# Four of thirty-two weight pieces converted in slots 21 and 22 of a fused attention and MLP kernel

## The chip, the cores and the metric

The kernel runs on one core of one Trainium2 chip. The metric is the device time of one execution in microseconds (us), as the median of several runs; lower is better. Beside it stands one profiled execution, recorded instruction by instruction.

## The reference, cut to what matters

```python
# q, k, v: (8, 8, 576, 64) float32; tau = 0.02
scores = (1 / sqrt(64)) * q @ k.transpose(0, 1, 3, 2)
thresh = max(scores, -1) - tau
scores = where(scores >= thresh, scores, -1e9)
attn = exp(scores - max(scores, -1))
attn = attn / (sum(attn, -1) + 1e-9)
x = (attn @ v) -> rows (b, s), columns (h, d): (4608, 512)
h = x @ w_in                 # (512, 2048), float64 as handed over
g = 0.5 * h * (1 + erf(h / sqrt(2)))
out = g @ w_out              # (2048, 512), float64 as handed over
```

The two weight matrices reach the kernel as 64-bit floats. [...] every weight element is turned from 64 to 32 bits on the chip, once, by integer operations on the two 32-bit halves of each number.

## The kernel before, in words

**Slots.** The attention is cut into pairs of heads: p = 0 to 31, four pairs to a batch. A pair has five score chunks, i = 0 to 4: four of 128 query rows for each of the two heads, and a last one (i = 4, `NC`) with the 64 rows left over from both. One chunk of one pair is a slot, n. Slots 0 to 7 hold chunks 0 and 1 of pairs 0 to 3, slots 8 to 19 their chunks 2 to 4, and from slot 20 (`BATCH`) on each pair has five slots in a row. The main loop (L1137 to L1257) goes through the slots and issues the instructions of each in an order written out by hand; nothing is reordered later, each engine works its own list from front to back.

**A slot.** `scores` (L391) puts four matmuls into two PSUM tiles `sc` (one tile when i = 4); there are two such tiles in all, so the scores of slot n+1 need the tiles of slot n to have been read. `softmax_head` (L403) has, for each of the two heads e, VectorE's row maximum `nmx` (L412), GpSimd's threshold `thr` (L415) and ScalarE's exponential `p` (L417). `softmax_tail` (L420) multiplies by the mask on VectorE (L433), which is also the last reader of `sc`. The probabilities are then turned. For the first four pairs TensorE does it (L347, copied out by ScalarE at L354 and L362); from slot 20 on VectorE does (L532 or L530), followed by DMAs that regroup (L550, L554). `turn_qk` (L372; L382, L383, L388 on VectorE), issued at i = 2, turns q and k of the next pair, after ScalarE scaled q (L370, at i = 1). `weigh_v` (L571) multiplies with v into `xT`; ScalarE copies it to a block of x (L589).

**The MLP between.** 256 rows of x make a block. `fill` (L695) puts matmuls of the MLP of blocks 0 to 7 into the slots as soon as there is credit for them: layer 1 (L671, `hT` from w_in), GELU on ScalarE, then layer 2 (L686, `o_ps` from `g` and w_out, j = 0 to 15 in turn, twice for the two halves of a block). A matmul is only issued when the weight pieces it needs have been converted in the program's order (`converted`, L707). Until slot 20 ScalarE only copies layer 1's results out (L638); the GELU of these, held back, runs in slot 20 (`gelus_held`, L648), and the first `o_ps` matmuls stand in slots 21, 22 and 23. The last ten blocks are done after the attention, with fewer multiplications (L859).

**Weight pieces.** There are 32 pieces of 128 x 512 elements (512 KB each, raw): 16 of w_in, then 16 of w_out, so that piece 16 + j is row block j of w_out. One conversion step of a piece is:

- an SP DMA that loads the raw piece (`load_piece`, L161), every second one into one of the seven x slots of `xall`, the others into `turned_p`, about eight pieces ahead;
- two ScalarE activations (`convert_first`, L196: `power` at L199 and the part in the weight at L200), done one piece ahead of the rest;
- two VectorE operations (`convert_second`, L203: L207 and L208), after which the next raw piece is loaded;
- one GpSimd addition (`add_low_bits`, L215, L219), which makes the weight ready. In the next slot it is issued for the newest piece between the first head's `nmx` and the first `thr` (L414), and for older pieces after the slot's head (L1144).

`STEPS` (L1129) says how many steps stand at the end of each slot (L1231); it adds up to 32 by slot 18. The tiles `power` come from the pool `gp` with ten buffers, which also holds `g`, the outputs of layer 1. Before the last slots of the first batch `convert_ahead` (L1173) issues ScalarE's part early. `LATER` is the number of last pieces that always go to x slots, because `turned_p` is needed for its own purpose from slot 20. `keep_busy` (L1239) adds a few idle matmuls in slots 1, 6 and 8.

## Time and profile before

| | |
|---|---|
| median of 3 runs | 1331.73 us (1331.51 to 1331.79) |
| the profiled execution's own time | 1331.37 us |
| its span | 1329.2 us |
| TensorE busy | 1315.9 us, 99% |
| VectorE busy | 1040.7 us, 78% |
| ScalarE busy | 604.3 us, 45% |
| GpSimd busy | 635.2 us, 48% |
| VectorE L207, one piece | median 423 ns, least 416, most 962 |
| VectorE L208, one piece | median 693 ns, most 1646 |
| ScalarE L199, one piece | about 705 ns |
| GpSimd L219, one piece | about 1272 ns |

The 2.2 us between the profiled execution's span and its own time lie outside the span. Busy times are sums over the whole span; the engines depend on each other, so the stretch that the change touches, from slot 2 (18.65 us after the start) to slot 24 (147 us), has to be looked at by itself. In the records two instructions that follow each other overlap a little: L207 and L208 take 0.42 and 0.69 us each, and two steps together 2.13 us. A 32-bit matmul shows as two records.

### The profile page before, as it was taken

The page shows a single profiled execution, that of the slowest core. Times are in us where ns is not written, and L with a number is a line of the kernel's source. Part 1 is how long each engine was busy: PE and PEld are TensorE (multiplying, and loading weights), DVE is VectorE, ACT ScalarE, POOL GpSimd, SP SyncE. Part 2 cuts the span into 40 slices and gives each one's busy share as a digit, 9 for nine tenths or more (in the row PEclk, how much of TensorE's full clock was granted, in tenths as well). Part 3 has the DMA queues.
Part 4 walks back from the last instruction along what each step waited for, and adds up shares of the span by engine and source line. Part 5 has one row for each costly group of instructions (what it writes and reads, how often), then busy time and mean ns, then how long its engine had stood idle before and what let it go on. Part 6 is the DMA issues. An engine that isn't in the chain of part 4 may idle for free.

```text
span 1329.2 us, 19865 instructions
## 1 busy us (share of the span) xinstructions
PE 1315.9 (99%) x6306; PEld 891.0 (67%) x6306; DVE 1040.7 (78%) x2001; ACT 604.3 (45%) x1027; POOL 635.2 (48%) x1058
## 2 busy tenths in 40 slices
PE   9999999999999999999999999999999999999998
PEld 6766466476476466466466466468778787877877
DVE  6887787788888888888888888883857698386674
ACT  7987356367367358358458338232111203211120
POOL 3555445555655655655655641236264403645430
PEclk9999999999999999999999999999999999999999
DMA  8553666777877887787787775500000140000003
GB/s 260 166 179 88 141 150 160 169 162 159 191 170 156 192 186 157 193 198 162 184 207 159 176 174 108 106 9 0 1 0 1 40 105 15 0 1 0 1 0 79
DMA packets 213687, 153.14 MB, mean 115 GB/s; under 512 B 117264, under 2 KB 196992, under 8 KB 213584
## 3 DMA queue, kind: packets, MB, share of 16 engines
q1 hardware_dynamic: 195440, 125.31, 40.7%
q0 software_dynamic: 17712, 26.26, 7.6%
q8 instruction: 52, 0.85, 0.3%
q14 instruction: 51, 0.42, 0.1%
q10 hardware_dynamic: 432, 0.30, 0.1%
HBM read 56.62 MB, written 12.58 MB: 52 GB/s over the span
## 4 chain that ended last, share of the span: by engine, by line
PE 93%; DVE 3%; ACT 2%; issue 1%; DMA 0%; POOL 0%; DVEq 0%; ACTq 0%; POOLq 0%
PE bank L859 34%; PE o_ps L686 17%; PE hT L671 16%; PE sc L400 13%; PE xT L571 11%; DVE nmx L412 1%; ACT p L417 1%; DVE power L208 1%; DVE p L433 1%; DVE power L207 1%; PE tr L347 1%; DMA q<-in_q_dram 0%; ACT pT L354 0%; PE tr L317 0%; PE idle L147 0%
## 5 line engine op out<-in xcount | busy, mean ns | idle before, releaser
L417 ACT ACTIVATE p<-sc,nmx 128x576 f32<-128x576 f32 x288 | 201.9, 737 | 280.9 <-DVE nmx L412 280.7
L433 DVE SCALAR_TENSOR_TENSOR p<-sc,thr,p 128x576 f32<-128x576 f32 x288 | 225.3, 816 | 72.6 <-ACT p L417 66.1
L415 POOL TENSOR_SCALAR thr<-nmx,tau_eff 128x1 f32<-128x1 f32 x288 | 83.9, 293 | 340.2 <-DVE nmx L412 338.1
L671 PE MATMUL hT<-xall,w_in 128*128 128x256 f32 x1024 | 241.9, 386 | 0.0
L412 DVE TENSOR_REDUCE nmx<-sc 128x1 f32<-128x576 f32 x288 | 205.4, 750 | 44.9 <-PE sc L400 43.7
L686 PE MATMUL o_ps<-w_out,g 128*128 128x512 f32 x512 | 236.8, 603 | 0.2 <-ACT g L644 0.2
L671 PEld LDWEIGHTS hT<-xall,w_in 128*128 128x128 f32 x1024 | 189.7, 190 | 51.1 <-issue 24.5
L741 DVE TENSOR_TENSOR o<-o,bank 128x256 f32<-128x256 f32 (+1 forms) x242 | 100.2, 418 | 94.3 <-PE bank L859 89.3
L741 DVE TENSOR_TENSOR c<-c,bank 128x320 f32<-128x320 f32 x304 | 147.1, 488 | 34.2 <-PE bank L859 21.0
L686 PEld LDWEIGHTS o_ps<-w_out,g 128*128 128x128 f32 x512 | 93.2, 190 | 109.5 <-issue 106.7
L400 PE MATMUL sc<-kT,qT 64*128 64x288 f32 x960 | 160.5, 429 | 1.9 <-DVE p L433 1.2
L571 PE MATMUL xT<-pT,v 128*64 128x320 f32 (+1 forms) x1240 | 159.4, 410 | 0.2
L532 DVE STREAM_TRANSPOSE turned_p<-p 128x1152 f32<-128x1152 f32 x112 | 154.4, 1378 | 3.9
L400 PEld LDWEIGHTS sc<-kT,qT 64*128 64x128 f32 x960 | 91.9, 186 | 75.8 <-issue 60.8
L571 PEld LDWEIGHTS xT<-pT,v 128*64 128x64 f32 x1240 | 86.4, 137 | 70.8 <-issue 11.1
L859 PE MATMUL bank<-w_out,c 128*128 128x256 f32 (+1 forms) x484 | 120.5, 380 | 0.8 <-DVE o L741 0.8
L260 POOL DMA_DIRECT2D v<-in_v_dram x208 | 110.8, 536 | 3.7 <-issue 1.6
L859 PEld LDWEIGHTS bank<-w_out,c 128*128 128x128 f32 x484 | 90.4, 190 | 18.8 <-DVE o L741 3.2
L926 ACT ACTIVATE c<-c 128x320 f32<-128x320 f32 (+1 forms) x80 | 46.9, 624 | 115.0 <-DVE c L741 114.9
L859 PE MATMUL bank<-t_out,g 128*128 128x256 f32 (+1 forms) x324 | 82.5, 377 | 0.4 <-DVE o L741 0.4
L859 PE MATMUL bank<-t_out,c 128*128 128x256 f32 x320 | 82.8, 381 | 0.0
L741 POOL TENSOR_TENSOR c<-c,g 128x320 f32<-128x320 f32 (+1 forms) x40 | 50.5, 1271 | 67.5 <-DVE c L741 67.5
(185 smaller groups left out, 1751.2 us busy)
## 6 DMA issues: line engine op xcount, KB each, us to landing
pT<-turned_p SPq DMA_DIRECT2D x448, 160.0 KB, 3.6
pT<-pd_tail SPq DMA_DIRECT2D x112, 80.0 KB, 3.0
q<-in_q_dram POOLq DMA_DIRECT2D x104, 72.0 KB, 3.6
k<-in_k_dram POOLq DMA_DIRECT2D x104, 72.0 KB, 3.3
inv<-turned SPq DMA_DIRECT2D x54, 128.0 KB, 4.1
v<-in_v_dram POOLq DMA_DIRECT2D x156, 40.0 KB, 3.1
out_dram<-o SPq DMA_DIRECT2D x40, 128.0 KB, 2.4
xall<-in_moe_w_out_dram SPq DMA_DIRECT2D x9, 512.0 KB, 4.7
```

The lines of the kernel that those rows point to most:

```text
L260: eng.dma_start(t[r:P:4, e, 0:n, :], rows[:, r * KR:r * KR + n, :])
L400: nc.tensor.matmul(sc[e][:, h, 0:HALF], lhsT=lhsT, rhs=s["kT"][rows, at:at + HALF], start=True, stop=True)
L412: nc.vector.tensor_reduce(nmx[:, e:e + 1], sc, axis=AXIS.XY, op=ALU.max, negate=True)
L415: nc.gpsimd.tensor_scalar(thr[:, e:e + 1], nmx[:, e:e + 1], -1.0, tau_eff, op0=ALU.mult, op1=ALU.subtract)
L417: nc.scalar.activation(w[:, e * S:(e + 1) * S].rearrange("p (h s) -> p h s", h=2), sc, AF.Exp, bias=nmx[:, e:e + 1], scale=1.0)
L433: nc.vector.scalar_tensor_tensor(row, sc[e][:, :, 0:HALF], thr[:, e:e + 1], row, op0=ALU.is_ge, op1=ALU.mult, accum_out=den[e])
L532: nc.vector.transpose(turned_p[:, :, i // 2, 0:NB, i % 2 * Q:(i % 2 + 1) * Q], w.rearrange("p (e b i) -> p e b i", e=2, i=Q))
L571: nc.tensor.matmul(to, lhsT=s["v"][:, e, c, :], rhs=rhs, start=(c == 0), stop=(c == KR - 1))
L671: nc.tensor.matmul(hT[:, j % 2, :], lhsT=w_in_sb[c][:, j * P:(j + 1) * P], rhs=x_blk[n][:, c, :], start=(c == 0), stop=(c == N_DM - 1))
L686: nc.tensor.matmul(o[:, 0:d_model], lhsT=g[j][:, m * P:(m + 1) * P], rhs=w_out_sb[j], start=(j == 0), stop=(j == N_DF - 1))
L741: eng.tensor_tensor(out, a, b, op=ALU.add)
L859: nc.tensor.matmul(to, lhsT=l, rhs=r, start=start and k == 0, stop=k == len(pairs) - 1, skip_group_check=not start)
```

## The change

It does four things. `STEPS` loses the step of slot 2 and that of slot 4, and one of the two steps in slot 6 and in slot 18; the other slots up to 18 keep their number. The four steps are put at the end of slots 21 and 22, two each; in these ScalarE's part is no longer done ahead (`ahead_of` = 0), so that each piece goes through its ScalarE and VectorE operations before the next one begins. `LATER` becomes 4: pieces 28 to 31 are loaded into x slots and stay raw there. `load_piece` remembers loads that found no free x slot and makes up for them later. In the program as built TensorE's list of instructions is the same before and after; the lists of the other engines differ in the places of the conversion steps and of their loads.

```diff
-    LATER = 2
+    LATER = 4
...
+    wanted = [0]
...
     def load_piece(eng=nc.sync):
-        k = loaded[0]
-        if k == len(pieces):
-            return
-        staged = k % 2 and k < len(pieces) - LATER
-        if wide and not staged and not x_free:
-            return
...
+        wanted[0] += 1
+        while wanted[0] > 0 and loaded[0] < len(pieces):
+            k = loaded[0]
+            staged = k % 2 and k < len(pieces) - LATER
+            if wide and not staged and not x_free:
+                return
...
+            wanted[0] -= 1
...
-    def convert(steps):
+    def convert(steps, ahead_of=1):
 
         while steps > 0 and (ahead or raws):
-            convert_ahead(1)
+            convert_ahead(ahead_of)
             convert_second()
             steps -= 1
...
-    STEPS = [0, 1, 1, 1, 1, 1, 2, 1, 2, 2, 2, 2, 3, 2, 2, 3, 2, 2, 2]
+    STEPS = [0, 1, 0, 1, 0, 1, 1, 1, 2, 2, 2, 2, 3, 2, 2, 3, 2, 2, 1, 0, 0, 2, 2]
...
-            convert_ahead(STEPS[n] if n < BATCH - 1 else LATER)
+            convert_ahead(STEPS[n])
...
-        convert(STEPS[n] if n < BATCH - 1 else len(pieces))
+        convert(STEPS[n] if n < len(STEPS) else 0, 1 if n < BATCH else 0)
```

More of the change, by code (lines that the diff above doesn't have):

```diff
@@ L155 @@
     wide = moe_w_in.dtype != FP32
-    LATER = 2
+    LATER = 4
     raws = []
     loaded = [0]
+    wanted = [0]
     converted = [0]
     def load_piece(eng=nc.sync):
-        k = loaded[0]
-        if k == len(pieces):
-            return
-        staged = k % 2 and k < len(pieces) - LATER
-        if wide and not staged and not x_free:
-            return
-        dst, src = pieces[k]
-        loaded[0] += 1
-        if not wide:
-            nc.sync.dma_start(dst, src)
-            converted[0] += 1
-            load_piece()
-            return
-        slot = []
-        if staged:
-            half, at = divmod(k // 2 % 4, 2)
-            raw = pd[half].bitcast(U32)[:, at * 2 * PIECE:(at + 1) * 2 * PIECE]
-        else:
-            slot = [x_slot()]
-            raw = x_rows(slot[0]).bitcast(U32)
-        eng.dma_start(raw, src.bitcast(U32))
-        raws.append((dst, raw, slot))
+        wanted[0] += 1
[4 more added lines that the diff above has]
+                return
+            dst, src = pieces[k]
+            loaded[0] += 1
+            if not wide:
+                nc.sync.dma_start(dst, src)
+                converted[0] += 1
+                continue
+            wanted[0] -= 1
+            slot = []
+            if staged:
+                half, at = divmod(k // 2 % 4, 2)
+                raw = pd[half].bitcast(U32)[:, at * 2 * PIECE:(at + 1) * 2 * PIECE]
+            else:
+                slot = [x_slot()]
+                raw = x_rows(slot[0]).bitcast(U32)
+            eng.dma_start(raw, src.bitcast(U32))
+            raws.append((dst, raw, slot))
     ahead = []
```

## The prediction

> **What bounds the kernel now.** I read the page first, then TensorE's busy time by stretch, then the timeline of the slots that the change touches. The page has TensorE at 99% over the span:

> ```profile
> PE 1315.9 (99%) x6306; PEld 891.0 (67%) x6306; DVE 1040.7 (78%) x2001; ACT 604.3 (45%) x1027; POOL 635.2 (48%) x1058
> ```

> So only time in which TensorE stands still can be won, and any new standstill is lost for good, because its list runs in a fixed order. Where it stands still is in the table of stretches (start and end in us, then busy time of TensorE, of its weight loads, VectorE, ScalarE, GpSimd):

> ```profile
> 42.00:60.00 18.00, 17.12 (x153) 13.12 (x153) 16.79 (x36) 16.60 (x37) 9.91 (x15) 1.00 0.49 159
> 60.00:80.00 20.00, 18.62 (x102) 13.45 (x101) 16.42 (x35) 17.18 (x35) 10.45 (x13) 1.00 0.52 138
> 100.00:118.00 18.00, 16.53 (x93) 11.64 (x92) 15.81 (x32) 14.20 (x30) 11.30 (x15) 1.00 0.52 136
> ...
> 130.00:141.00 11.00, 11.00 (x31) 4.89 (x30) 6.67 (x12) 7.67 (x13) 5.10 (x11) 1.00 0.28 61
> 141.00:147.00 6.00, 6.00 (x19) 2.73 (x19) 5.71 (x12) 1.41 (x2) 3.64 (x8) 1.00 0.99 191
> ```

> From 42 to 118 us (slots 7 to 18) VectorE and ScalarE are nearly as full as TensorE and TensorE has gaps. From 130 us on (slots 21 to 24) TensorE has none, and in the last row VectorE is busy 5.71 of 6 us: slots 22 and 23 have no room on VectorE. Slots 2 to 6 are another case. In TensorE's own table it works 16.91 of 17 us there:

> ```profile
> 25.00:42.00 17.00, 16.91 (x168) 1.00 0.76 268
> ```

> The timeline shows slot 6 passing into slot 7 on VectorE (start, length):

> ```profile
> 42.81 0.42 DVE L207 TENSOR_SCALAR power<-power 128x512 uint32<-128x512 uint32 x1
> 43.27 0.69 DVE L208 SCALAR_TENSOR_TENSOR power<-turned_p,power 128x512 uint32<-128x512 uint32 x1
> 43.88 0.42 DVE L207 TENSOR_SCALAR power<-power 128x512 uint32<-128x512 uint32 x1
> 44.33 0.69 DVE L208 SCALAR_TENSOR_TENSOR power<-xall,power 128x512 uint32<-128x512 uint32 x1
> 44.94 1.42 DVE L412 TENSOR_REDUCE nmx<-sc 128x1 f32<-128x576 f32 x2
> ```

> Two steps cost 44.94 - 42.81 = 2.13 us, 1.06 each, and the maximum follows without a gap: here VectorE sets the pace. And slots 21 to 24:

> ```profile
> 135.11 0.82 DVE L433 SCALAR_TENSOR_TENSOR p<-sc,thr,p 128x576 f32<-128x576 f32 x1 [4.08 <-ACT p L417]
> 136.71 1.38 DVE L532 STREAM_TRANSPOSE turned_p<-p 128x1152 f32<-128x1152 f32 x1
> 137.95 2.84 PE L686 MATMUL o_ps<-w_out,g 128*128 128x512 f32 x6
> 138.01 1.39 DVE L412 TENSOR_REDUCE nmx<-sc 128x1 f32<-128x576 f32 x2
> 140.72 1.79 PE L400 MATMUL sc<-kT,qT 64*128 64x288 f32 x8
> 141.20 1.38 DVE L532 STREAM_TRANSPOSE turned_p<-p 128x1152 f32<-128x1152 f32 x1
> 142.45 4.56 PE L686 MATMUL o_ps<-w_out,g 128*128 128x512 f32 x10
> 144.24 1.42 DVE L412 TENSOR_REDUCE nmx<-sc 128x1 f32<-128x576 f32 x2
> 146.84 1.21 PE L400 MATMUL sc<-kT,q_tail 128*128 128x288 f32 x4
> ```

> VectorE idled 4.08 us (a wait for ScalarE, which runs the held-back GELUs) and then has no gap up to 145.6. Slot 23's scores take 1.79 us where eight such records take 1.24 elsewhere: they wait on VectorE's mask already.

> [...] nothing fills VectorE's 4.08 us from behind the waiting mask. [...] L207 has a median of 423 ns and took 962 at 48.24 us, beside a GpSimd multiplication. [...] the largest gap of TensorE between 42 and 160 us is 0.9 us, at clock 1.00.

> **The change part by part.**

> *Slots 2 and 4, one step less each.* VectorE's two operations (21.96 to 23.03 in slot 2) lie in front of a maximum that starts at 23.48 and waits for TensorE's scores (22.20 to 23.44). ScalarE's part (24.16 to 25.31) holds slot 3's exponential back by about 1.0 us, but what that releases, slot 4's scores, stands behind `xT`, `tr` and transposes that keep TensorE busy from 23.53 to 29.1. Slot 4 repeats it (`xT` at 34.05, scores at 38.42). Value: 0. Bounds: 0 to 0.4 us, the small gaps in the records from 21 to 42 us; it cannot be a loss, since work only leaves.

> *Slot 6, two steps to one.* The maximum of slot 7 could start at 43.88, but its scores (43.19, behind the idle matmuls) allow it 1.27 us after their start, as in slots 3 and 5 (22.20 to 23.48, 32.73 to 34.00): 44.46, won 0.48. Then GpSimd: in slot 7 it has one addition instead of two (1.27 us). The first, at 45.17, held the threshold until 46.42 and the mask until 46.76, 1.82 after the maximum; an undelayed mask comes 1.64 after it (39.69 to 41.33). The addition now ends at 45.4: mask at 46.10, won 0.66. The second held the multiplication L498 until 48.18, and this L207 for 0.96 us instead of 0.42. Now L498 can end near 47.7, L207 and L208 at 48.7, and slot 8's maximum starts at 48.75 instead of 49.84. The scores permit it: they wait for the mask too. Won by slot 8: 1.1 us. From there to slot 17 every slot keeps its number of steps, and the gaps above are waits on VectorE, ScalarE and GpSimd, so all move forward together: 1.1 us. Bounds: 0.4 (only the first part) to 1.8 (about one more such collision in ten slots).

> *Slot 18, two steps to one.* VectorE's part (117.21 to 118.28) ended 0.57 us before the next maximum, which waited on TensorE's scores. ScalarE still converts one piece there ahead of the copies (115.79, piece 28 instead of 31), so TensorE's 0.91 us wait for `pT` stays. Value 0, bounds 0 to 0.3.

> *Loads and raw pieces.* Their SP loads keep their sequence and their distance to use. The last is issued behind the q, k and v loads of pair 5, which SP issues from 110.7 to 120.8; such a load lands in about 4.7 us and is used near 143. The four x slots held are seven less the three blocks of batch 0; the next block needs one in slot 27, at 164. Cost 0.

> *Slot 21, two steps added.* After the transpose of 136.71, at 138.01, come 2.13 us of steps (ScalarE's part for the second, 1.15 us, runs from 136.3 on an engine idle until 138.76). The maximum of slot 22 moves from 138.01 to 140.14. The addition for the newest piece, 1.27 us, starts with it, so the mask follows after 1.75 instead of 1.6: 141.9 to 143.4. Slot 23's scores need it and end at 144.7 instead of 142.45: TensorE has six records (2.84 us) in slot 22 and stands still for 2.3 us.

> *Slot 22, two steps added.* From the transpose at 143.5 on, the 3.04 us that lie between 141.20 and 144.24 (L532 and q and k of the next pair) and then 2.13 of steps: maximum of slot 23 at 148.7. ScalarE's parts, waiting for additions until about 143.5, take 2 x 1.15 and end at 145.8, before VectorE reaches them at 146.5. On GpSimd the addition for piece 31 takes 148.9 to 150.1, two thresholds 0.5, and only then comes the one for piece 30: 150.6 to 151.9. TensorE's ten records in slot 23 are j = 11 to 15, two each at 0.43; after j = 13 (147.3) it waits for piece 30 (j = 14) until 152.0. Behind it in TensorE's list are j = 15 and slot 24's scores: these start at 152.0 + 4 x 0.43 = 153.7 instead of 146.84. Delay 6.9 us. VectorE then is on time, so the 0.7 us that slot 25's scores (150.56) lose to a mask falls away: 6.2. GpSimd's k, q and v loads for pair 6 move back some 4 to 5 us; they are used five slots later: 0.

> Bounds of the loss: 4 (additions beside other work, half the last wait) to 7.5 (a VectorE and GpSimd collision in each slot). Apart from that, TensorE stands still for 4.7 us in one piece. [...] I take 0 and keep up to 3 for the range.

> *Sum:* 6.2 - 1.1 = 5.1 us. Against the profiled execution: 1329.2 + 5.1 + 2.2 outside the span = 1336.5. Its 1331.37 lies 0.36 under the median of 1331.73, so in medians 1336.8.

> **The rivals.**

> *The clock falls* in the 4.7 us gap: the same, and about 2.7 more, 1339.5. [...]

> *The last addition isn't what TensorE waits for.* Then slot 24's scores wait for the mask of slot 23 alone, near 151.3: 4.5 - 0.7 - 1.1 = 2.7, 1334.4, on the border to no change. For: one order on GpSimd decides. Against: thresholds stand before that addition in its list.

> *The steps are hidden (faster).* VectorE idles 4.08 us before 135.11. If the 2 x 2.13 us of steps fell into that, or TensorE had work queued beyond the next scores, nothing would be lost and 1.1 to 2 us won: 1330.2. The place is slot 22: it decides if TensorE's work there (2.84 us) is longer than VectorE's way from one scores to the next. It is not: 138.01 to 141.09 was already 3.1 us. Against it also the fixed order: the steps stand behind the mask that waits.

> *The change moves less than it says.* If TensorE's list had been rearranged around the late pieces, layer 2 would simply come later. The built program's list is unchanged, so the waits are real: 1331.7 otherwise.

> **How the numbers follow.** About 0.2% (2.7 us) is what a measurement of this kernel can tell from no change. Forecast 0.60; clock falls 0.18; border case 0.12, half of it slower; hidden 0.05; no effect 0.05. Slower: 0.60 + 0.18 + 0.06 = 0.84; same: 0.06 + 0.05 = 0.11; faster 0.05. The range runs from 1333.8 (loss of 4, gain of 1.8) to 1340.0 (loss of 6.2 to 7.5 with a fallen clock); the two left-out cases, and the ends of the others, are under 2 in 10.

> **What would show it.** The maximum of slot 8 near 48.75; slot 20 earlier by about 1.1. In slots 21 to 24, moved forward by that: TensorE idle about 2 us before slot 23's scores (released by VectorE L433) and 4 to 5 us in slot 23's `o_ps` (released by GpSimd's addition), the rest of the kernel unchanged but later by 5. I am wrong if that second wait is under 2 us, if slot 8 has not moved, or if the early slots 2 to 6 move by over half a microsecond.

## The result, and the profile after

Times are medians of the runs of one chip; the kernel before was run beside the other each time.

| | before | after |
|---|---|---|
| median, us (lowest to highest, runs) | 1331.64 (1330.61 to 1331.79, 6) | 1337.89 (1336.92 to 1339.11, 6) |
| ratio to before, 95% interval | 1 | 1.0049 [1.0036, 1.0062] |
| profiled execution, us | 1331.37 | 1337.85 |
| span, us | 1329.2 | 1335.9 |
| mean granted TensorE clock | 0.999 | 0.997 |

The change costs 6.25 us; the forecast was 5.1 us (1336.8), the range 1333.8 to 1340.0. All line numbers of the kernel after are one higher than before (L412 is L413).

The page's line of busy times says almost nothing: TensorE is at 99% in both, and its sum has risen by 3.1 us. The fall of the clock shown further down is of that size: about 3.2 us.

```profile
PE 1319.0 (99%) x6306; PEld 890.5 (67%) x6306; DVE 1039.1 (78%) x2001; ACT 604.8 (45%) x1027; POOL 635.7 (48%) x1058
```

**The early part.** TensorE by stretch, kernel after (start and end, then busy time of TensorE, weight loads, VectorE, ScalarE, GpSimd; near the end the clock):

```profile
25.00:42.00 17.00, 16.92 (x168) 12.41 (x164) 11.89 (x26) 14.53 (x33) 7.29 (x14) 1.00 0.60 220
42.00:60.00 18.00, 17.60 (x158) 13.99 (x158) 16.49 (x36) 16.46 (x36) 8.76 (x14) 1.00 0.37 117
60.00:80.00 20.00, 18.23 (x100) 13.09 (x99) 16.07 (x33) 16.22 (x33) 10.46 (x13) 1.00 0.54 144
```

Slots 3 to 6 are where they were (16.92 of 17 us against 16.91). From 42 to 60 us TensorE has 0.48 us less of gaps, and from 60 to 80 us it has 0.39 us more again. VectorE's timeline shows the gain arise. Before:

```profile
46.76 0.82 DVE L433 SCALAR_TENSOR_TENSOR p<-sc,thr,p 128x576 f32<-128x576 f32 x1 [0.33 <-POOL thr L415]
...
48.24 0.96 DVE L207 TENSOR_SCALAR power<-power 128x512 uint32<-128x512 uint32 x1
49.23 0.69 DVE L208 SCALAR_TENSOR_TENSOR power<-turned_p,power 128x512 uint32<-128x512 uint32 x1
49.84 1.41 DVE L412 TENSOR_REDUCE nmx<-sc 128x1 f32<-128x576 f32 x2
```

After:

```profile
44.47 1.42 DVE L413 TENSOR_REDUCE nmx<-sc 128x1 f32<-128x576 f32 x2 [0.51 <-PE sc L401]
...
46.10 0.82 DVE L434 SCALAR_TENSOR_TENSOR p<-sc,thr,p 128x576 f32<-128x576 f32 x1
...
47.59 0.62 DVE L208 TENSOR_SCALAR power<-power 128x512 uint32<-128x512 uint32 x1
48.24 0.69 DVE L209 SCALAR_TENSOR_TENSOR power<-xall,power 128x512 uint32<-128x512 uint32 x1
48.84 1.41 DVE L413 TENSOR_REDUCE nmx<-sc 128x1 f32<-128x576 f32 x2
```

The maximum of slot 7 now waits for the scores (44.47; forecast 44.46), the mask is at 46.10 (as forecast), L208 (L207 before) takes 0.62 us, with a GpSimd multiplication (L499) beside it up to 47.92, instead of 0.96 with the same one (L498 before) beside it up to 48.92, and slot 8's maximum is at 48.84 instead of 49.84.

**Slots 21 to 24.** TensorE's timeline (start, length, and in brackets the idle time before the group and what ended it):

```profile
137.32 2.84 PE L687 MATMUL o_ps<-w_out,g 128*128 128x512 f32 x6
142.26 3.00 PE L401 MATMUL sc<-kT,qT 64*128 64x288 f32 x8 [2.10 <-DVE p L434]
145.18 5.00 PE L687 MATMUL o_ps<-w_out,g 128*128 128x512 f32 x6
151.38 1.98 PE L687 MATMUL o_ps<-w_out,g 128*128 128x512 f32 x4 [1.20 <-POOL w_out L220]
153.20 1.13 PE L401 MATMUL sc<-kT,q_tail 128*128 128x288 f32 x4
```

Two standstills that the kernel before did not have: 2.10 us for VectorE's mask, 1.20 us for the addition on GpSimd. Slot 24's scores stand at 153.20 instead of 146.84. GpSimd's own list shows the order that makes the second one: the addition for piece 31, two thresholds, and only then the one for piece 30.

```profile
148.28 1.26 POOL L220 TENSOR_TENSOR w_out<-power,w_out 128x512 uint32<-128x512 uint32 x1 [1.66 <-DVE power L209]
149.53 0.57 POOL L416 TENSOR_SCALAR thr<-nmx,tau_eff 128x1 f32<-128x1 f32 x2
150.07 1.25 POOL L220 TENSOR_TENSOR w_out<-power,w_out 128x512 uint32<-128x512 uint32 x1
```

And the stretches show something that the profile before has nowhere between its first and its last microseconds: the granted clock (third number from the end) falls.

```profile
140.00:142.00 2.00, 0.16 (x1) 0.00 (x0) 1.59 (x3) 1.75 (x3) 2.00 (x4) 1.00 0.94 174
142.00:143.00 1.00, 0.74 (x3) 0.33 (x3) 0.97 (x5) 0.98 (x3) 1.00 (x2) 0.87 0.91 236
143.00:149.00 6.00, 6.00 (x12) 2.92 (x12) 5.89 (x11) 1.20 (x3) 4.34 (x7) 0.50 0.60 140
149.00:150.00 1.00, 1.00 (x2) 0.10 (x1) 0.59 (x2) 1.00 (x2) 1.00 (x3) 0.72 0.00 0
```

Half clock from 142.73, just after the first standstill, for 6.83 us. That is why six `o_ps` records took 5.00 us instead of 2.84 and slot 23's scores 3.00 us: TensorE looks busy from 143 to 149 (6.00 of 6 us), but at a granted clock of 0.50.

**Where the time is.** Start of a slot's scores on TensorE, after minus before:

| slot | 0 | 8 | 9 | 12 to 22 | 23 | 24 | 26 | 81 | 111 | 131 |
|---|---|---|---|---|---|---|---|---|---|---|
| us | +0.04 | -0.46 | -1.00 | -0.63 | +1.53 | +6.36 | +5.64 | +5.94 | +6.10 | +6.77 |

So 1.0 us is won by slot 9, 0.63 of it kept; 6.99 us is lost from slot 22 to slot 24, 0.72 comes back by slot 26; and 1.1 us more slips in later, in slots whose instructions the change does not touch.

### The profile page after: what moved, and what is told of

Read it like the earlier page. It is cut to its first block, busy times and chain, and to the rows that moved or that the text cites. A ratio compares the mean times of both kernels' runs of the same rounds, so it can differ in the third digit from the quotient of the medians.

```text
span 1335.9 us, 19863 instructions
## 1 busy us (share of the span) xinstructions
PE 1319.0 (99%) x6306; PEld 890.5 (67%) x6306; DVE 1039.1 (78%) x2001; ACT 604.8 (45%) x1027; POOL 635.7 (48%) x1058
## 4 chain that ended last, share of the span: by engine, by line
PE 89%; DVE 3%; ACT 3%; DMA 2%; issue 1%; SPq 1%; POOL 1%; DVEq 0%; POOLq 0%; ACTq 0%
PE bank L860 34%; PE hT L672 16%; PE o_ps L687 15%; PE sc L401 12%; PE xT L572 10%; ACT p L418 1%; DVE nmx L413 1%; DMA inv<-turned 1%; PE tr L348 1%; DVE p L434 1%; DMA turned<-turned 1%; ACT pT L355 0%; DVE power L209 0%; DVE power L208 0%; DVE turned_p L533 0%
## 5 line engine op out<-in xcount | busy, mean ns | idle before, releaser
L413 DVE TENSOR_REDUCE nmx<-sc 128x1 f32<-128x576 f32 x288 | 205.3, 749 | 53.0 <-PE sc L401 51.8
```

The source lines that it names most:

```text
L413: nc.vector.tensor_reduce(nmx[:, e:e + 1], sc, axis=AXIS.XY, op=ALU.max, negate=True)
```

## The experiments

Three theories are tested. *The wait (A):* the steps at the end of slots 21 and 22 fill VectorE and GpSimd, TensorE waits for the mask and for the last addition, and the half clock lies under that wait and costs nothing. *The clock (B):* the fall of the clock is part of the cost. *The x slots (C):* four raw pieces kept in x slots press on what comes later. Unless said otherwise an edit is made to the kernel after. Profiles do not all start alike (slot 0 lies up to 0.7 us earlier or later); where it matters the offset is taken off, and said.

**e1: the first standstill filled.** Twelve records of idle matmuls at the end of slot 22.

```diff
-    BUSY = {1: 2, 6: 2, 8: 2}
+    BUSY = {1: 2, 6: 2, 8: 2, 22: 3}
```

> The changed kernel with twelve records of idle matmuls (1.7 us) at the end of slot 22, where TensorE waits 2.1 us for the mask. They should hold the clock at 1.00 there. Theory A (TensorE's start of slot 24 is set by VectorE's steps and then by the last GpSimd addition, and the half clock is hidden under that wait): o_ps of slot 23 takes 2.6 to 2.9 us for its first six records instead of 5.0, the wait for the addition grows from 1.2 to about 4 us, slot 24's scores start within 0.4 us of 153.2, and the total stays within 0.1% of the changed kernel's 1337.9, or up to 2 us above it if the longer wait brings the clock down later. Theory B (the half clock is what costs beyond the mask): slot 24 starts 2 us earlier or more, total 1336 or less.

Measured: 1339.97 us (1338.66 to 1341.31), ratio 1.0059 [1.0044, 1.0074]. TensorE's timeline:

```profile
140.41 1.50 PE L298 MATMUL idle<-ident 128*128 128x128 f32 x12
142.68 1.95 PE L401 MATMUL sc<-kT,qT 64*128 64x288 f32 x8 [0.77 <-DVE p L434]
144.55 2.84 PE L687 MATMUL o_ps<-w_out,g 128*128 128x512 f32 x6
151.80 3.78 PE L687 MATMUL o_ps<-w_out,g 128*128 128x512 f32 x4 [4.41 <-POOL w_out L220]
155.38 2.13 PE L401 MATMUL sc<-kT,q_tail 128*128 128x288 f32 x4
```

At full clock the six `o_ps` records take 2.84 us, and the wait for the addition is 4.41 us, not 1.20. So the second wait was there in the kernel after, too: the half clock had stretched the matmuls in front of it into it. The sum agrees: (3.00 - 1.95) + (5.00 - 2.84) = 3.21 us, and 4.41 - 1.20 = 3.21 us. But here the clock fell in the second standstill (147.39 to 151.80; half clock from 150.63, for 6.83 us), and nothing covers what comes behind it: four records take 3.78 us instead of 1.98, and slot 24 stands 1.8 us later than in the kernel after (8.53 less 0.43 of offset, against 6.32).

**e2: both standstills filled.** As e1, and 20 records of idle matmuls before j = 14 of slot 23.

```diff
+    if n == 0 and m == 0 and j == 14:
+        keep_busy(5)
...
-    BUSY = {1: 2, 6: 2, 8: 2}
+    BUSY = {1: 2, 6: 2, 8: 2, 22: 3}
```

> The changed kernel with twelve records of idle matmuls at the end of slot 22 and twenty (2.9 us) ahead of j = 14 in slot 23, so that both waits of TensorE are filled and the clock should stay at 1.00 throughout. Theory A (the delay is VectorE's and GpSimd's; the clock adds to it only where it falls in the open): slot 24's scores start as late as in the changed kernel, within 0.4 us of 153.2, and the total is 1337 to 1338; less spread between runs than in the kernel with the first filling alone, and about 2 us faster than it. Theory B (the clock costs the time): 1335 or less.

Measured: 1338.41 us (1337.4 to 1339.3), ratio 1.0049 [1.0035, 1.0063]; in the profile the clock stays at 1.00 from 6.96 us until 1.7 us before the end.

```profile
144.46 2.84 PE L689 MATMUL o_ps<-w_out,g 128*128 128x512 f32 x6
147.14 2.39 PE L298 MATMUL idle<-ident 128*128 128x128 f32 x20
151.72 1.98 PE L689 MATMUL o_ps<-w_out,g 128*128 128x512 f32 x4 [2.18 <-POOL w_out L220]
153.54 1.13 PE L401 MATMUL sc<-kT,q_tail 128*128 128x288 f32 x4
```

Slot 24 is 6.69 us late, less 0.27 of offset 6.42: the same as in the kernel after (6.32), without any fall. The loss is made by VectorE and GpSimd alone, as A has it, and where the fall lies under the wait it costs nothing. Slot 24 starts 1.7 us sooner than in e1, where the fall lay in the open; the medians point the same way (6.7 us over the kernel before, against 7.9 in e1), with overlapping intervals.

**e3: both additions ahead of the thresholds in slot 23.**

```diff
+                if (p, i) == (HP, 3):
+                    add_low_bits(True)
```

> The changed kernel with both GpSimd additions of slot 23 ahead of the first threshold. Theory A: piece 30 is ready near 150.8 minus 0.5, so before TensorE has come to it (150.2 at the half clock) or just about; the wait of 1.2 us falls to under 0.3, but the mask comes 1.2 us later (151.1 to 152.6); slot 24's scores start near 152.2 instead of 153.2, total about 1 us less than the changed kernel, 1336.9. Theory B (the clock sets the time): no change in the start of slot 24 beyond 0.2 us. A third view, that the mask and not the addition is last: slot 24 starts later by about 1 us.

Measured: 1337.23 us (1336.23 to 1339.54), ratio 1.0036 [1.0024, 1.0049]. The wait for the addition is 3.85 us where it is 4.4 with full clock otherwise; it ends 0.6 us sooner (150.30 plus 0.46 of offset, against 151.38). The expected wait of under 0.3 us took over the half clock of the profile after; in this run the clock held through the first standstill. The medians lie 0.7 us under the kernel after, with overlapping intervals; in the profile the order of the two additions is worth about what the two thresholds take (0.57 us). The clock fell here, too, from 151.62 for 3.41 us.

**e4: nothing in slot 22.** Pieces 28 and 29 before the mask of slot 21 (VectorE's 4.08 us of idle time in the kernel before), 30 and 31 at the end of slot 21.

```diff
-    STEPS = [..., 3, 2, 2, 3, 2, 2, 1, 0, 0, 2, 2]
+    STEPS = [..., 3, 2, 2, 3, 2, 2, 1, 0, 0, 2, 0]
+    MID = {21: 2}
+    AHEAD = {19: 1}
...
-        if long:
-            convert_ahead(STEPS[n])
+        if long or n in AHEAD:
+            convert_ahead(AHEAD.get(n, STEPS[n]))
...
+        for _ in range(MID.get(n, 0)):
+            convert_second()
+        if n in MID:
+            add_low_bits()
```

> The changed kernel, with pieces 28 and 29 converted in the middle of slot 21, ahead of its mask, where VectorE idles 4.1 us, and pieces 30 and 31 at the end of slot 21; nothing in slot 22. Theory A: slot 23's scores are late by 2.1 to 2.3 us as in the changed kernel, slot 24 by about 2.3 less the early gain, and of that 0.7 comes back at slot 25; total against the kernel before +1.0 us, 1332.6 (range 1331.8 to 1334, the top if the clock falls for 6.8 us as it did after the same gap of 2.1 us: half of six records and more is then lost in the open). Theory B (clock): the top of that range or above, since nothing hides the half clock here: 1335.

Measured: 1336.15 us (1332.6 to 1338.29, 11 runs), ratio 1.003 [1.0021, 1.0039]: above the range that A was given. The profile is of a run that took 1333.57 us:

```profile
141.78 1.94 PE L401 MATMUL sc<-kT,qT 64*128 64x288 f32 x8 [2.17 <-DVE p L434]
143.65 4.56 PE L687 MATMUL o_ps<-w_out,g 128*128 128x512 f32 x10
148.04 1.21 PE L401 MATMUL sc<-kT,q_tail 128*128 128x288 f32 x4
```

The first standstill is the same 2.2 us, the second is gone, the clock did not fall, and slot 24 is 1.20 us late (1.7 with the offset). The eleven times lie in two groups: 1332.6 and 1333.57, with a mean granted clock of 0.999, and nine from 1335.37 to 1338.29, with 0.996 or 0.997. Half clock for 6.83 us lowers the mean of such a run by 0.0026, so the clock fell in the nine. With no second wait to hide it the fall costs about 3 us (the nine have a median of 1336.23, the two a mean of 1333.1): here B has its part. That it fell after this standstill fits, but is not seen, since only one run has a profile.

**e5: nothing at the end of slot 21, two steps in slot 22.** The rest as in e4.

```diff
-    STEPS = [..., 3, 2, 2, 3, 2, 2, 1, 0, 0, 2, 2]
+    STEPS = [..., 3, 2, 2, 3, 2, 2, 1, 0, 0, 0, 2]
+    MID = {21: 2}
+    AHEAD = {19: 1}
```

> The changed kernel, with pieces 28 and 29 converted in the middle of slot 21 and pieces 30 and 31 at the end of slot 22; nothing at the end of slot 21. Theory A: no wait before slot 23's scores (under 0.3 us), then one long wait of 4 to 5 us for the addition for piece 30 in slot 23 at clock 1.00; slot 24 late by 4.6 less the early gain of 0.6, 0.7 back at slot 25: total against the kernel before +3.3 us, 1334.9 (up to 1338 if the clock falls after that gap, since it is nowhere hidden). Theory B: no long wait.

Measured: 1336.36 us (1335.57 to 1337.76), ratio 1.0033 [1.0021, 1.0045].

```profile
140.44 1.80 PE L401 MATMUL sc<-kT,qT 64*128 64x288 f32 x8
142.17 2.84 PE L687 MATMUL o_ps<-w_out,g 128*128 128x512 f32 x6
149.41 2.88 PE L687 MATMUL o_ps<-w_out,g 128*128 128x512 f32 x4 [4.40 <-POOL w_out L220]
```

Here the first standstill is gone and the second is whole; slot 24 is 5.23 us late (4.8 with the offset), 0.9 of it because the clock fell from 150.36 for 3.41 us (2.88 us for 1.98). So in the profiles slot 22's pair of late steps is the dearer, 3.9 us without the fall against 1.7 in e4. In the medians the two come out alike, because most runs of e4 have a fall in the open.

**e6: slots 2 and 4 alone.** Steps as before except none in slots 2 and 4; the two last pieces go before the mask of slot 21, by the lines of e4 (so in e7 to e12 as well).

```diff
-    LATER = 4
+    LATER = 2
...
-    STEPS = [0, 1, 0, 1, 0, 1, 1, 1, 2, 2, ..., 2, 2, 1, 0, 0, 2, 2]
+    STEPS = [0, 1, 0, 1, 0, 1, 2, 1, 2, 2, ..., 2, 2, 2, 0, 0, 0, 0]
+    MID = {21: 2}
+    AHEAD = {18: 1, 19: 1}
```

> The kernel before with the steps of slots 2 and 4 taken out, and the two last pieces converted in the middle of slot 21, in VectorE's 4.1 us of idling. Theory A (slots 2 to 6 are bound by TensorE): slot 7 and slot 8 start within 0.2 us of before, the total is within 0.4 us of before. Rival (each step taken out of an early slot wins its 1.06 us of VectorE): 2.1 us faster. Also: the kernels built from the changed one lose about 1.1 us between slots 80 and 131; if that comes with the four x slots kept raw, it is not seen here.

Measured: 1331.91 us (1330.54 to 1332.89, 13 runs), ratio 1.0000 [0.9992, 1.0008]; the slots' starts are within 0.2 us of those before. The steps of slots 2 and 4 are worth nothing, and two pieces before slot 21's mask cost nothing that shows.

**e7: slot 6 alone.** One step less in slot 6, the last piece before the mask of slot 21.

```diff
-    LATER = 4
+    LATER = 2
...
-    STEPS = [0, 1, 0, 1, 0, 1, 1, 1, 2, ..., 2, 2, 1, 0, 0, 2, 2]
+    STEPS = [0, 1, 1, 1, 1, 1, 1, 1, 2, ..., 2, 2, 2, 0, 0, 0, 0]
+    MID = {21: 1}
+    AHEAD = {}
```

> The kernel before with one of the two steps of slot 6 taken out, and the last piece converted in the middle of slot 21. Theory A: slot 7 starts 0.5 us earlier, slot 8 1.0 us earlier; of this 0.6 to 1.0 is kept to slot 24 and to the end, total 0.6 to 1.0 us faster (ratio 0.9993 to 0.9995). Rival (the step in slot 6 is hidden as those in 2 and 4): no change.

Measured: 1333.11 us (1332.07 to 1334.22, 13 runs), ratio 1.0010 [1.0002, 1.0019]: slower, a miss. The edit had a flaw: in slot 18 it put two pieces through ScalarE ahead of the copies of `pT`, not one, and TensorE waited for these:

```profile
117.32 0.33 PE L348 MATMUL tr<-ident,p 128*128 128x128 f32 x1 [2.05 <-ACT pT L355]
```

That is 2.05 us instead of 0.91, and the clock fell to half at 118.29 for 3.41 us. A fault of the experiment, but a second place where the fall came after a standstill of 2 us.

**e10: slot 6 again, mended.** All else as e7.

```diff
-    AHEAD = {}
+    AHEAD = {18: 1}
```

> The experiment with slot 6 alone, mended: in slot 18 only one piece goes through ScalarE ahead of the copies of pT, as in the kernel before; the last piece follows at the end of that slot, where ScalarE idles 1.5 us. Theory A: TensorE's wait for pT in slot 18 is 0.9 us again instead of 2.1, the clock doesn't fall there, slot 8 starts 1.0 us earlier and the total is 0.6 to 1.0 us under the kernel before. If the total stays above before, the gain of slot 6 is lost elsewhere.

Measured: 1330.78 us (1329.85 to 1331.82, 21 runs), ratio 0.9989 [0.9983, 0.9996], 1.6 us faster by medians, more than the 0.6 to 1.0 expected. The wait for `pT` is back at 0.9 us, the clock stays; in the profile slot 9 is 1.0 us earlier (0.39, and 0.6 of offset), kept to the end. The gain of slot 6 is real, and in the profile close to the 1.1 us of the forecast.

**e8: slots 6 and 8, one step less each.** Two pieces before the mask of slot 21.

```diff
-    LATER = 4
+    LATER = 2
...
-    STEPS = [0, 1, 0, 1, 0, 1, 1, 1, 2, 2, ..., 2, 2, 1, 0, 0, 2, 2]
+    STEPS = [0, 1, 1, 1, 1, 1, 1, 1, 1, 2, ..., 2, 2, 2, 0, 0, 0, 0]
+    MID = {21: 2}
+    AHEAD = {18: 1, 19: 1}
```

> The kernel before with one of the two steps taken out of each of slots 6 and 8, and the two last pieces converted in the middle of slot 21. Theory A: VectorE sets the pace in slot 8 as well, so a second 1.06 us comes on top: slot 9 about 2 us earlier, total 1.6 to 2.1 us faster than before. Rival (the second step runs into TensorE's or ScalarE's bound): as with slot 6 alone, 0.6 to 1.0.

Measured: **1329.46 us** (1329.11 to 1330.38, 17 runs), ratio 0.9984 [0.9976, 0.9991], against 1331.75 for the kernel before: 2.3 us faster, and faster than both kernels of the case.

```profile
42.00:60.00 18.00, 18.00 (x163) 14.62 (x162) 15.61 (x33) 15.69 (x34) 8.82 (x14) 1.00 0.35 111
...
141.00:147.00 6.00, 6.00 (x16) 2.79 (x16) 5.61 (x11) 2.05 (x4) 3.00 (x7) 1.00 0.81 179
```

TensorE has no gap left from 42 to 60 us, and none in the late slots. Slot 12 is 2.6 us earlier (0.5 of it offset).

**e12: slots 6, 8 and 9.** As e8, with one step less in slot 9 too, put at the end of slot 19 with its addition at once.

```diff
-    STEPS = [..., 1, 1, 1, 2, 2, 2, 3, 2, 2, 3, 2, 2, 2, 0, 0, 0, 0]
+    STEPS = [..., 1, 1, 1, 1, 2, 2, 3, 2, 2, 3, 2, 2, 2, 1, 0, 0, 0]
...
+        if n == BATCH - 1:
+            add_low_bits()
+            convert_ahead(1)
```

> The kernel before with one of two steps taken out of each of slots 6, 8 and 9; one of the three goes to slot 19, where VectorE idles 3.2 us waiting for TensorE, with its addition at once, and two to the middle of slot 21. Theory A: a third 1.06 us on top of the experiment with slots 6 and 8 (2.3 us), total 3 to 3.4 us faster than before. Rival (ScalarE's two parts in slot 19 delay the copies and slot 20's exponential): no more than the 2.3 us of slots 6 and 8.

Measured: 1330.12 us (1329.33 to 1331.8, 19 runs), ratio 0.9982 [0.9975, 0.9989]: in ratio the same as e8. Slot 12 is 2.45 us earlier, slot 22 2.18; the third step brings nothing that shows, where 3 to 3.4 us in all were expected. In e8 TensorE has no gap left up to 60 us; and in the profile of e12 later slots slip to -0.8 us by slot 131.

**e11: four raw pieces in x slots, nothing else.** The kernel after with the steps of before.

```diff
-    STEPS = [0, 1, 0, 1, 0, 1, 1, 1, 2, 2, 2, 2, 3, 2, 2, 3, 2, 2, 1, 0, 0, 2, 2]
+    STEPS = [0, 1, 1, 1, 1, 1, 2, 1, 2, 2, 2, 2, 3, 2, 2, 3, 2, 2, 2, 0, 0, 0, 0]
```

> The kernel before with the last four pieces loaded into x slots instead of the last two, every step where it was. Theory C (the kernels with four raw x slots lose 1.1 to 1.5 us in waits for DMAs between slots 80 and 131, and the four slots are why): 0.8 to 1.5 us slower than before, with later starts near slots 81, 111 and 131. Theory A alone (the loads cost nothing, these waits are chance of the run): within 0.4 us of before.

Measured: 1332.31 us (1330.96 to 1333.13, 13 runs) against 1332.37, ratio 0.9999 [0.9991, 1.0007]. C falls as far as loading four pieces into x slots goes; here all pieces are converted by slot 18, so keeping the slots until slot 22 is not tested by itself. Yet its profile, with an offset of 0.64 at slot 0, has slot 91 at +1.11 and slot 131 at +1.32: late slips come without any late step.

**e13: the changed kernel once more,** with no edit.

> The changed kernel once more, for a second profile and more times. Theory A: slot 24 late by 6.2 to 6.5 us against before, 5.4 to 5.8 at slot 26; whether the clock falls in the wait of slot 22 (hidden) or of slot 23 (in the open, up to 2 us more) differs between runs and makes the spread of 2 us. Total 1337 to 1339.5.

Measured: 1338.05 us (1336.95 to 1339.28), ratio 1.0043 [1.0031, 1.0056]. TensorE's timeline, the same program as after:

```profile
141.81 1.94 PE L401 MATMUL sc<-kT,qT 64*128 64x288 f32 x8 [2.10 <-DVE p L434]
143.68 2.84 PE L687 MATMUL o_ps<-w_out,g 128*128 128x512 f32 x6
150.93 3.68 PE L687 MATMUL o_ps<-w_out,g 128*128 128x512 f32 x4 [4.41 <-POOL w_out L220]
154.45 1.13 PE L401 MATMUL sc<-kT,q_tail 128*128 128x288 f32 x4
```

Both standstills are those of after (2.10 us, and 4.41 at full clock), but this time the clock held through the first and fell in the second, from 151.01 for 3.41 us. Slot 24 is 8.1 us late once the offset of -0.46 is taken off, 1.7 us more than in the profile of after. So where the fall comes differs from run to run and moves one run by nearly 2 us; it is a part of the spread from 1336.9 to 1339.3.

The traces show where the falls lie. In five profiles the granted clock fell a whole multiple of 3.413 us after it first reached 1.00: at 6.14 and 1327.10 us in before (387 times, at the end of the work), at 6.20 and 142.73 in after (40), at 4.24 and 151.01 in e13 (43), at 7.27 and 150.63 in e1 (42), at 5.65 and 118.29 in e7 (33). TensorE's idle time in single steps of this raster:

| run | stretch, us | TensorE idle, us | clock behind it |
|---|---|---|---|
| after | 139.32 to 142.73 | 2.10 | half |
| e7 | 114.88 to 118.29 | 2.05 | half |
| e3 | 148.20 to 151.62 | 2.10 | half |
| e5 | 143.54 to 146.95, then to 150.36 | 1.94, then 2.46 | full, then half |
| e1 | 147.21 to 150.63 | 3.23 | half |
| e4 | 138.15 to 141.56 | 1.96 | full |
| e13 | 137.36 to 140.78, then to 144.19 | 1.07, then 1.05 | full, full |
| e13 | 147.60 to 151.01 | 3.33 | half |

In these rows the clock fell behind 2.05 us idle or more of 3.41 and stayed at 1.00 behind 1.96 or less. In before and after no other step at full clock has more than 1.20 us idle, and full clock follows each, but for the step in which the matmuls end: 2.70 us idle in both, half clock behind it. In after the first standstill lay whole in one stretch; in e13 a border cut it in two. A wait of 4.41 us can't be laid over this raster without 2.2 us or more of it in one step; so if these rows hold for other runs, which is an estimate, the clock falls in every run of the kernel after, in one wait or in the other. The mean clocks agree: 0.996 to 0.998 in all six runs and in the five of e13, against 0.999 in the profile before. The 1.96 and 2.05 us were read off afterwards; no run was built to test them.

## Why the prediction was right, point by point

**The loss, 6.2 us: right, step by step.** The forecast was worked out without the early gain. Adding the 0.63 us by which the slots were earlier in fact:

| step | forecast | measured + 0.63 |
|---|---|---|
| mask of slot 22, first | 141.9 | 141.91 |
| TensorE stands before slot 23's scores | 2.3 us | 2.10 us |
| maximum of slot 23 | 148.7 | 148.68 |
| addition for piece 31 | 148.9 | 148.91 |
| addition for piece 30 | 150.6 to 151.9 | 150.70 to 151.95 |
| j = 14 on TensorE | 152.0 | 152.01 |
| slot 24's scores | 153.7 | 153.83 |
| given back by slot 26 | 0.7 us | 0.72 us |

The VectorE and GpSimd queues set every one of these times, and each instruction in them took about what its row of before had shown. Net of what is given back, the loss is 6.27 us. That the sum met this profile so closely is in part luck: the fall of the clock, put at 0, lay under the wait here, and in e13 it did not.

**The second wait: right in time, wrong in look.** The forecast said TensorE would stand 4.7 us for the addition, and that it would be wrong were the wait under 2 us. In the profile after it is 1.20 us. By that test the step failed; the reason is the step "I take 0" for the clock. The waits view of after, as it stands, would lead astray:

```profile
PE sc L401 <- DVE p L434: 2.1, 1, 2.1
PE o_ps L687 <- POOL w_out L220: 1.2, 1, 1.2
```

3.3 us of waiting for a delay of 7.0: of the missing 3.7 us, 3.2 are in matmuls that run at half clock up to the wait (the sum under e1); the rest is in small stretches of the groups around the gaps. The end of the wait was set by GpSimd and did not move. e1, e2, e5 and e13 show the wait whole where those six records ran at full clock (4.41, 2.18 after 2.39 us of idle matmuls, 4.40, 4.41).

**The clock: it fell, where the rival did not look.** The rival had it fall in the second gap, of 4.7 us. In the profile after it fell after the first, 2.10 us long. The rival's weight of 0.18, its 2.7 us and the forecast's "up to 3" for the clock were the author's estimates; no run had shown them, since in the profile before the clock is at 1.00 from 6.14 to 1327.10 us. What the runs show is under e13: a raster of 3.413 us, and a place of the fall that varies between two runs of the same program (142.73 in after, 151.01 in e13). The clock fell behind 2.05 us idle in one step (e7), and stayed at 1.00 behind 1.96 (e4). So it was wrong to look at the second gap alone: a standstill of 2.10 us was followed by the fall, too. In cost the forecast of 0 held for the profile after, and failed for e13 (1.7 us); the "up to 3" held both.

**Slots 2 and 4, 0 us: right** (e6: ratio 1.0000).

**Slot 6, 1.1 us kept up to slot 17: right in size at slot 9, not kept whole.** 1.00 us was won by slot 9 and 0.63 remained from slot 12 on. The step that failed is "all move forward together". The timeline of slot 10 shows where: GpSimd's addition starts 0.51 us after the VectorE and ScalarE operations before it have ended (60.24), where before the distance was 0.15 us (61.25 to 61.40).

```profile
59.55 0.69 DVE L209 SCALAR_TENSOR_TENSOR power<-xall,power 128x512 uint32<-128x512 uint32 x1
59.56 0.68 ACT L201 ACTIVATE w_in<-turned_p 128x512 uint32<-128x512 uint32 x1
...
60.75 1.27 POOL L220 TENSOR_TENSOR w_in<-power,w_in 128x512 uint32<-128x512 uint32 x1 [2.58 <-DVE power L209]
```

Before:

```profile
61.40 1.27 POOL L219 TENSOR_TENSOR w_in<-power,w_in 128x512 uint32<-128x512 uint32 x1 [2.23 <-DVE power L208]
```

This is no chance of one run: the distance is 0.47 to 0.51 us in all seven profiles of the kernels with this order of steps up to slot 12 (after, e1 to e5, e13), and each loses the same 0.35 to 0.38 us between slots 11 and 12. In e10, with the step taken out of slot 6 alone, it is 0.14 us, and the 1.0 us was kept. So it comes with the program; by what it comes is open.

**Slot 18, loads and x slots, 0: nothing speaks against it.** e11 shows the four loads into x slots at 0; the wait for `pT` in slot 18 is not a cause of the difference in any kernel but e7.

**The end.** The forecast had "the rest of the kernel unchanged". After minus before: 6.48 us in the profiled executions, of which 5.1 was forecast; 0.5 is the part of the early gain that was not kept, 0.1 the loss (6.27 for 6.2), and some 0.8 are slips after slot 26 (1.1 us in the starts of the slots, of which 0.3 does not reach the execution's own time). The step that failed is "unchanged". Part of it comes with the program: from slot 26 to slot 81 all seven profiles of the kernels named above slip by 0.30 to 0.34 us, and so does e12; in the other five changed kernels it is 0.02 at the most. What sets it is open. The largest slip, 0.67 us by slot 131, is another matter: e13, the same program, has none there. It goes with a wait in GpSimd's timeline. After:

```profile
687.70 1.69 POOL L620 TENSOR_TENSOR xall<-xall,inv 128x128 f32<-128x128 f32 x3 [0.84 <-DMA inv<-turned]
689.33 2.16 POOL L261 DMA_DIRECT2D v<-in_v_dram  x4
691.53 0.31 POOL L416 TENSOR_SCALAR thr<-nmx,tau_eff 128x1 f32<-128x1 f32 x1
```

Before, the same three without the wait:

```profile
680.77 1.69 POOL L619 TENSOR_TENSOR xall<-xall,inv 128x128 f32<-128x128 f32 x3
682.40 2.16 POOL L260 DMA_DIRECT2D v<-in_v_dram  x4
684.70 0.31 POOL L415 TENSOR_SCALAR thr<-nmx,tau_eff 128x1 f32<-128x1 f32 x1
```

The multiplication waited 0.84 us for `inv`, whose loads were issued 4.41 us after the store that they read, against 3.24 us before; the issue of the v loads and then a threshold stand behind it. The instructions there are the same in both kernels. That this wait makes the slip is not shown: e7 has 4.37 us at the same place and next to no slip (0.06 us by slot 131). That this part is chance is likely, not shown.

## What to carry to other kernels

Before work is moved to a later place, walk each engine's list there from one due time to the next: the 4.08 us in front of slot 21's mask took two steps for nothing, while two steps one slot later, in a list without a gap, made the bound engine stand still for 4.4 us (e5), because its next matmul needed their result. Work taken away from a full stretch pays only as far as the bound engine has gaps there (slots 6 and 8: 2.3 us; slots 2 and 4, and slot 9 as a third: nothing). And when the sum of the waits is less than the delay, look at the clock by stretch: a matmul at half clock counts as busy (6.00 of 6 us at 0.50 here), and it can make a wait look short that is as long as ever (1.20 us in after, 4.41 in e1).
